# Filter, squared-ReLU layer and slot dispatch on one core: the row path of the dispatch issued later, batch 2 loaded later, probe matmuls left out

## The chip, the cores and the metric

One Trainium2 chip, one of its cores. The metric is the device time of the program in microseconds (us); each run is one execution.

## What is computed

```python
X = np.fft.rfft(x, axis=1); Y = X * F[None]          # x: 8 x 3072 x 256
y = np.fft.irfft(Y, n=3072, axis=1)                  # 24576 tokens x 256
h = np.maximum(y @ w_in, 0.0)                        # 256 -> 2048
z = h * h @ w_out                                    # 2048 -> 256
logits = z @ phi                                     # 24576 x 32 slots
d = softmax of logits over the tokens; slot_input = d.T @ z
slot_out[e] = relu(slot_input[e] @ w1[e]) @ w2[e]    # 8 experts, 4 slots each
c = softmax of logits over the slots
out = c @ slot_out
```

The softmax over all 24576 tokens is kept running: a maximum, a sum and a rescaled accumulator. The softmax over the slots (here the row path) is finished for each token as soon as its logits are there.

## The kernel before

**Filter.** The transform of a batch is split as 128 x 24. The first stage (`mm_a`, `evac_a`, `store_a`) writes its result S to DRAM; the filter stage (`mm_b`, then products on VectorE in `filt` and sums on GpSimd in `join`) and the inverse stage (`mm_g2`, `evac_g2`, `store_g2`) write G to DRAM. `load_g` reads G into `gin`, `mm_ai` transforms and transposes four token columns, and `lead_ai` (ScalarE) and `rest_ai` (VectorE) leave them in `xo` as a leading part and a residual. Batch 0 runs alone at the start; batches 1 to 7 run beside the layer of the batch before.

**Layer.** Work goes in 384 pairs of hidden tiles, eight pairs to a chunk of 512 tokens. A pair has two halves; a half is six matmuls (L460 to L462, three for each of two contraction tiles) into one bank, p0 or p1, which has no second buffer. `square` frees the bank with a relu on ScalarE (L467). The square itself is ScalarE's for the first half (L469) and GpSimd's for the second (L471). `turn_h` transposes both halves into `hT` on VectorE (L478), and `logit` (L487) sums h times a folded weight into bank L every two pairs.

**Dispatch**, once a chunk of tokens (48 times, `dispatch_events`). `evac_l` copies the logits, `gather` sums them into a bank X, `emax` takes the running maximum (VectorE: mn L542, nm L545), `expo` the exponentials (ScalarE: et L551, sc L554), `turn_l` transposes the logits (lt L562) and releases X, `turn_e` transposes the exponentials (eT L568), `slot_in` multiplies them with `hT` into four banks (L589), and `accum` adds these to the accumulator (ac L605, z L612). The row path is `row_max` (rm L574, cl L575), `row_exp` (ScalarE: ce L596), `row_out` (sm, co L623 to L626) and `store_c`.

**What sets the order.** Everything is issued in the order of the Python code. `pair(P)` runs four quarter steps at the times 2P, 2P + 0.5, 2P + 1 and 2P + 1.5, so a time unit is half a pair. Each step first runs events that need no bank, then three matmuls (after two steps the half's `square`), then the other events that are due. Events lie in streams (dsp for the dispatch, late for `out_events`, fft for the filter) with a time each, and leave a stream in that order:

```python
        def put(t, fn, *a):
            streams[nm].append((t + o, fn, a))
...
                if te > t or (n and (early or hold)):
                    break
                if n > len(free):
```

Five side banks are shared by gather, slot_in, the filter's stages and mm_ai; an event that finds too few holds back those behind it. In a dispatch chunk c the times start from `q = 16 * (c + 1) + 2`. An engine's queue runs in the order of issue, and so does SP's, which issues nearly all DMAs. For batch b the times of the filter come from `when`: the first stage's start and spacing, then the starts of the four filter-stage and the four inverse-stage groups, counted from 96 (b - 1).

At the start, beside batch 0, `warm` and `probe` issue matmuls on constants whose results are not read.

Of the kernel before, what the change touches and what calls it, by code (L numbers as in the profile page):

```python
# [6 lines left out]
F32 = mybir.dt.float32  # L7
F32R = mybir.dt.float32r
# [30 lines left out]
def body(tc, x, cA, cAf, fwd, inv, flt, cst, w_in, w_out, phi, w1, w2, out):  # L39
    nc = tc.nc  # L40
    sync = nc.sync
    act, vec, gps, pe = nc.scalar, nc.vector, nc.gpsimd, nc.tensor

    def pool(name, bufs=1, space=None, side=None):
        kw = {} if space is None else {"space": space}
        p = tc.tile_pool(name=name, bufs=bufs, side=side, **kw)
        return p, p.__enter__()
# [7 lines left out]
    cv_c, cv = pool("cv")  # L55
# [43 lines left out]
    def side():  # L99
        if G["nsd"]:  # L100
            return G["ps"].tile([128, 512], F32, tag="sd", name="sd", bufs=G["nsd"])
        k = free.pop(0)
        p = G["ps"].tile([128, 512], F32, tag=f"s{k}", name="sd")
        taken[id(p)] = k, p
        return p
# [7 lines left out]
    def fft_events(b, pl, put, A0, dA, TB, TG, n, st):  # L113
# [190 lines left out]

        def load_ca():
            vec.memset(st["wz"], 0.0)
            gps.memset(st["wy"], 0.0)
            sync.dma_start(out=st["ca"], in_=cAf)

        def warm(a, n):  # L310
# [3 lines left out]
            for _ in range(n):  # L314
                pe.matmul(p[:, 0:w], a[:, 0:128], a, start=True, stop=True)

        def probe():

            m = st["wz"].bitcast(F32R)
            w = st["wy"].bitcast(F32R)  # L320
            p, p2 = side(), side()
            for a, cols, count in ((w, 512, 10), (m, 512, 6), (w, 256, 12), (w, 384, 6), (w, 128, 12)):
                for _ in range(count):
                    pe.matmul(p[:, 0:cols], a[:, 0:128], m[:, 0:cols], start=True, stop=True)
            for _ in range(4):
                for r, q in enumerate((p, p2)):
                    rows = slice(64 * r, 64 * r + 64)
                    pe.matmul(
                        q, w[rows, 0:128], m[rows, :], start=True, stop=True, tile_position=(64 * r, 0)
                    )  # L330

        if b == 0:

            st["wy"] = cv.tile([128, 128], F32, name="wy", bufs=1)
            st["wz"] = cv.tile([128, 512], F32, tag="wx", name="wz", bufs=1)
            st["ca"] = pl().tile([128, 128], F32, name="ca")
            put(0, load_ca)
            put(0.05, warm, st["wz"], 2)
            put(0.05, warm, st["wz"][:, 0:256], 1)
            put(18.2, warm, st["ca"], 16)  # L340
            put(18.25, probe)
            for sl in range(6):
                put(0.1 * sl + 0.2, load_x, sl)
            for u in range(12):
                put(4.6 + 0.9 * u, mm_a, u)
                put(6.7 + 1.0 * u, evac_a, u)
            for i in range(8):
                T = ST["B0"] + ST["dB"] * i
                put((.7, .75, 15)[i] if i < 3 else T - 6.5, load_c, i)
                put((.8, 9, 15.5)[i] if i < 3 else T - 6.4, load_f, i)  # L350
                put(18 + .1 * i if i < 3 else T - 6, load_s, i)
                put(T, mm_b, i)
                for r in range(2):
                    put(T + 1 + .5 * r, filt, i, r)
                    put(T + 1 + .5 * r, join, i, r)
                put(T + 5, mm_g, i)
                for c in range(4):
                    put(T + 6, evac_g, i, c)
                put(T + 7, store_g, i)
            return  # L360
# [157 lines left out]
    def dispatch_events(c, put):  # L518
        q = 16 * (c + 1) + 2
        st = {}  # L520
# [114 lines left out]
            return evac_l, gather, emax, expo, turn_e, turn_l, slot_in, accum, row_max, row_exp, row_out, store_c  # L635
        put(q + .5, evac_l)
        put(q + 1.5, gather)
        put(q + 2, emax)
        put(q + 2.5, expo)
        put(q + 3.5, turn_l)  # L640
        put(q + 4, turn_e)
        put(q + 4.5, row_max)
        put(q + 5.5, row_exp)
        put(q + 7, row_out)
        put(q + 7.5, slot_in)
        for r in range(4):
            put(q + 9 + .5 * r, accum, r)
        put(q + 13, store_c)


    def f64(t, a, e):
# [122 lines left out]
    def stream(nm, o=0):  # L774
        def put(t, fn, *a):
            streams[nm].append((t + o, fn, a))
        return put
# [67 lines left out]
    with tc.manual_schedule():  # L845
        put, late = stream("fft"), stream("late")
        st = {}
        put0(38, load_const)
        fft_events(0, lambda: first, put0, 0, 0, 0, 0, dict(f=17, u=12, c=4), st)
        out_events(0, st, late)  # L850
        def wput(t, *a):
# [22 lines left out]
        for b in range(1, NB):  # L874
            st = {}
            if b == 1:
                when = (24, 1.1, [45.5, 53.5, 65.5, 77.5], [49.5, 61.5, 69.5, 81.5])
            else:
                when = (-25, 1.5, [1.5, 21.5, 37.5, 53.5], [17.5, 33.5, 49.5, 65.5])
            fft_events(b, lambda: G["fft"], stream("fft", 96 * (b - 1)), *when, dict(f=3, u=8, c=2), st)  # L880
            out_events(b, st, late)
        for c in range(NCH - 1):
            dispatch_events(c, stream("dsp"))
# [4 lines left out]
        for P in range(NP + 2):  # L888
            if P == 9:
                open_fft()  # L890
            if P == 48 * (NB - 1):
                G["fft_c"].__exit__(None, None, None)
                G["w1_c"], w1p = pool("w1p")
                for n in range(6):
                    m = 4 if n < 5 else 2
# [25 lines left out]
        def bank(tag):  # L921
            return G["ps"].tile([128, 512], F32, tag=tag, name="pt")
# [28 lines left out]
        def go(*fns):  # L951
            for fn in fns:
# [3 lines left out]
                cnt[fn.__name__] = g + 1  # L956

        evac_l, gather, emax, expo, turn_e, turn_l, slot_in, accum, row_max, row_exp, row_out, store_c = dispatch_events(NCH - 1, None)
        zt = mlp.tile([128, NE, 8, NS], F32, tag="xo", name="zt", bufs=2)
        gps.memset(zt, 0.0)  # L960
# [18 lines left out]
        for n in range(4):  # L979
            w = NB * N2 // 4  # L980
# [14 lines left out]
        p = bank("s0")  # L995
        for j in range(16):
# [3 lines left out]
                start=(j < 4), stop=(j >= 12), tile_position=(0, 32 * c4),  # L1000
# [3 lines left out]
        p = bank("s1")  # L1004
# [61 lines left out]
        p = bank("s4")  # L1066
# [13 lines left out]
        for g in range(NG):  # L1080
            b, o = divmod(g, N2 // 4)
# [3 lines left out]
            for h in range(2):  # L1085
                p = bank(("s0", "s1", "s2", "s3")[ops % 4]).rearrange("p (a d) -> p a d", d=D)
# [156 lines left out]
```

## Time and profile before

| What | before |
|---|---|
| three runs, median (lowest to highest) | 2109.94 us (2109.88 to 2111.64) |
| profiled execution, its own time | 2109.53 us |
| its span, first to last instruction | 2107.3 us |
| busy: PE, DVE, ACT, POOL | 1975.0, 1231.4, 1044.5, 734.2 us |
| mean granted TensorE clock, share of full | 0.970 |
| DMA | 238.30 MB, mean 113 GB/s |

PE is TensorE's matmuls, DVE VectorE, ACT ScalarE, POOL GpSimd, SP the engine that issues the DMAs. Busy time is time in which an engine executes; idle time in front of an instruction is put down to what ended it. The granted clock has two levels, 1.00 (2.4 GHz) and 0.50 (1.2 GHz); a mean between them says how much of a stretch was at either. PE's records overlap, since matmuls are pipelined: a 512-column matmul is recorded with 0.39 us while its successors start 0.23 us apart.

### The profile page before, as it was taken

To read this page: it belongs to the slowest core of one execution; us is meant where nothing else is said; L and a number is where in the kernel's file an instruction comes from. 1 tells how busy PE (TensorE), PEld (TensorE's weight loads), DVE (VectorE), ACT (ScalarE), POOL (GpSimd) and SP (SyncE) were. 2 spreads that over 40 slices of the span, in tenths; PEclk is the share of its full clock that TensorE was granted. 3 is DMA by queue.
4 is the path that set the end of the run, shared out by engine and by line. 5 is a ranking of instruction groups with operands and counts; after the bars stand their busy time and mean duration, and the time that the engine had idled before them with its cause. 6 is when DMAs were issued, how large, how long until landed. Compare 5 with 4: busy or idle time off the path is not lost.

```text
span 2107.3 us, 44638 instructions
## 1 busy us (share of the span) xinstructions
PE 1975.0 (94%) x18364; PEld 1329.6 (63%) x18364; DVE 1231.4 (58%) x2276; ACT 1044.5 (50%) x1956; POOL 734.2 (35%) x787
## 2 busy tenths in 40 slices
PE   7799989999999999999999999999999999999987
PEld 4376656666666667666666667656666666666546
DVE  3674655665565655666466565566466565555548
ACT  2355545544644446445645446444654444444435
POOL 2424444333433334333433343333433332222224
PEclk8699999999999999999999999999999999999999
DMA  9744444241442324232343324223334213000479
GB/s 278 221 135 137 110 146 146 71 108 46 133 110 71 101 77 137 71 87 66 122 112 80 96 82 137 71 75 79 117 100 97 79 51 132 14 22 14 144 268 381
DMA packets 144539, 238.30 MB, mean 113 GB/s; under 512 B 14160, under 2 KB 96592, under 8 KB 144336
## 3 DMA queue, kind: packets, MB, share of 16 engines
q1 hardware_dynamic: 144048, 235.25, 37.5%
q8 instruction: 145, 2.38, 0.5%
q14 instruction: 58, 0.48, 0.1%
q0 software_dynamic: 288, 0.20, 0.0%
HBM read 154.65 MB, written 80.74 MB: 112 GB/s over the span
## 4 chain that ended last, share of the span: by engine, by line
PE 59%; DVE 14%; ACT 10%; issue 2%; POOL 0%; ACTq 0%; POOLq 0%; DVEq 0%
PE p L460 11%; PE p L462 10%; PE p L461 10%; PE sd L589 9%; PE L L487 8%; DVE hT L478 5%; PE sd L406 4%; ACT h L467 3%; ACT f L212 2%; PE sd L202 2%; ACT h L469 2%; DVE u L263 2%; DVE lt L562 2%; ACT et L551 1%; DVE mn L542 1%
## 5 line engine op out<-in xcount | busy, mean ns | idle before, releaser
L478 DVE STREAM_TRANSPOSE hT<-h 128x512 f32<-128x512 f32 x768 | 516.0, 695 | 427.0 <-ACT h L469 425.4
L471 POOL TENSOR_TENSOR h<-h 128x512 f32<-128x512 f32 x383 | 399.1, 1042 | 977.9 <-ACT h L467 872.3
L460 PE MATMUL p<-xo,wiH 128*128 128x512 f32 x1536 | 643.9, 419 | 71.6 <-ACT h L467 70.9
L467 ACT ACTIVATE h<-p 128x512 f32<-128x512 f32 x768 | 453.8, 595 | 514.2 <-PE p L462 492.8
L461 PE MATMUL p<-xo,wiH 128*128 128x512 f32 x1536 | 615.3, 401 | 0.2 <-DVE xo L427 0.2
L462 PE MATMUL p<-xo,wiL 128*128 128x512 f32 x1536 | 614.9, 400 | 0.0
L460 PEld LDWEIGHTS p<-xo,wiH 128*128 128x128 f32 x1536 | 292.8, 191 | 232.7 <-ACT h L467 114.2
L462 PEld LDWEIGHTS p<-xo,wiL 128*128 128x128 f32 x1536 | 293.5, 191 | 71.5
L461 PEld LDWEIGHTS p<-xo,wiH 128*128 128x128 f32 x1536 | 294.2, 192 | 57.2 <-DVE xo L427 0.8
L469 ACT ACTIVATE h<-h 128x512 f32<-128x512 f32 x385 | 243.4, 632 | 12.3
L605 DVE SCALAR_TENSOR_TENSOR ac<-ac,sc,sd 128x512 f32<-128x512 f32 x188 | 132.3, 725 | 180.9 <-PE sd L589 180.9
L272 POOL TENSOR_TENSOR u<-u 128x256 f32<-128x256 f32 x256 | 183.8, 742 | 143.8 <-DVE u L263 135.2
L589 PE MATMUL sd<-hT,eT 32*32 32x512 f32 x6144 | 216.6, 604 | 2.9 <-DVE eT L568 2.9
L487 PE MATMUL L<-h,wf 128*32 128x512 f32 x1536 | 190.9, 609 | 0.4 <-ACT h L469 0.4
L263 DVE TENSOR_TENSOR u<-sd,f 128x512 f32<-128x512 f32 x256 | 161.6, 677 | 29.3 <-PE sd L252 23.0
L589 PEld LDWEIGHTS sd<-hT,eT 32*32 32x32 f32 x6144 | 102.3, 103 | 113.2 <-issue 61.2
L137 POOL TENSOR_TENSOR u<-f,u 128x512 fp32r<-128x512 f32 x84 | 108.3, 1290 | 128.7 <-ACT u L136 119.6
L529 DVE TENSOR_TENSOR lo<-L,lp 128x512 fp32r<-128x512 f32 x48 | 33.1, 690 | 136.4 <-ACT lp L528 136.4
L406 PEld LDWEIGHTS sd<-cst_t,gin 128*128 128x128 f32 x768 | 101.0, 192 | 17.7 <-issue 6.8
L406 PE MATMUL sd<-cst_t,gin 128*128 128x128 f32 x768 | 102.1, 276 | 8.2 <-DMA gin<-G 8.2
L487 PEld LDWEIGHTS L<-h,wf 128*32 128x32 f32 x1536 | 40.8, 112 | 102.8 <-issue 100.9
L212 ACT ACTIVATE f<-sd 128x512 f32<-128x512 f32 x112 | 61.3, 611 | 88.5 <-PE sd L202 88.5
(118 smaller groups left out, 1528.7 us busy)
## 6 DMA issues: line engine op xcount, KB each, us to landing
f<-flt SPq DMA_DIRECT2D x28, 1024.0 KB, 5.7
f<-x SPq DMA_DIRECT2D x48, 512.0 KB, 4.2
S<-u SPq DMA_DIRECT2D x96, 256.0 KB, 2.1
f<-S SPq DMA_DIRECT2D x128, 192.0 KB, 7.3
G<-f SPq DMA_DIRECT2D x128, 192.0 KB, 3.2
gin<-G SPq DMA_DIRECT2D x48, 512.0 KB, 5.2
out<-w1t SPq DMA_DIRECT2D x47, 512.0 KB, 5.1
wx<-w SPq DMA_DIRECT2D x34, 256.0 KB, 5.3
```

The costliest lines, as they stand in the source:

```text
L263: vec.tensor_tensor(out=u, in0=p.rearrange("p (h d) -> p h d", d=D), in1=f[:, 2 * r + k:2 * r + k + 1, :].to_broadcast([128, 2, D]), op=AL ...
L272: gps.tensor_tensor(out=a[:, h, :], in0=a[:, h, :], in1=b[:, 1 - h, :], op=ALU.add if h else ALU.subtract)
L406: pe.matmul(p[:, 128 * a:128 * a + 128], t[:, a, 128 * k:128 * k + 128], cI, start=True, stop=True,)
L460: pe.matmul(p, wh, x[:, 0, kk, :], start=(kk == 0), stop=False)
L461: pe.matmul(p, wh, x[:, 1, kk, :], start=False, stop=False)
L462: pe.matmul(p, wl, x[:, 0, kk, :], start=False, stop=(kk == 1))
L467: act.activation(out=h, in_=p, func=ACTF.Relu, scale=2.0 ** -8)
L469: act.activation(out=h, in_=h, func=ACTF.Square)
L471: gps.tensor_tensor(out=h, in0=h, in1=h, op=ALU.mult)
L478: vec.transpose(hT[c][:, 2 * i + k, :], h2[P, k])
L487: pe.matmul(lg[c][32 * n:32 * n + 32, :], wf[:, f, :], h2.pop((P + n // 2, n % 2)), start=(f < 4), stop=(f >= FT - 4), tile_position=(0, 3 ...
L589: pe.matmul(S[r][32 * t:32 * t + 32, :], e[rows, o:o + 32], h[rows, :, o:o + 32], start=(a == 0), stop=(a == 3), tile_position=(32 * r, 32 ...
```

## The change

Three things are changed.

- In each of the 47 dispatch chunks that run beside the layer, `emax` moves from q+2 to q+2.5, `expo` from q+2.5 to q+3.5, `turn_l` from q+3.5 to q+4, `turn_e` from q+4 to q+5.5; `row_max` from q+4.5 to q+11, `row_exp` from q+5.5 to q+13, `row_out` from q+7 to q+14, `store_c` from q+13 to q+17. `slot_in` and `accum` stay.
- Batch 2 (the third) gets times of its own: its first stage starts at -14 with one step a unit instead of -25 and one in 1.5, and with it its loads of x; its first filter-stage group is at 5.5 instead of 1.5. Of batch 1 the last filter-stage group moves from 77.5 to 76.5 and the third inverse-stage group from 69.5 to 70.5.
- The 54 matmuls of `probe` and the tile they use are left out.

```diff
@@ -304,7 +304,6 @@
 
         def load_ca():
             vec.memset(st["wz"], 0.0)
-            gps.memset(st["wy"], 0.0)
             sync.dma_start(out=st["ca"], in_=cAf)
 
         def warm(a, n):
@@ -314,31 +313,14 @@
             for _ in range(n):
                 pe.matmul(p[:, 0:w], a[:, 0:128], a, start=True, stop=True)
 
-        def probe():
-
-            m = st["wz"].bitcast(F32R)
-            w = st["wy"].bitcast(F32R)
-            p, p2 = side(), side()
-            for a, cols, count in ((w, 512, 10), (m, 512, 6), (w, 256, 12), (w, 384, 6), (w, 128, 12)):
-                for _ in range(count):
-                    pe.matmul(p[:, 0:cols], a[:, 0:128], m[:, 0:cols], start=True, stop=True)
-            for _ in range(4):
-                for r, q in enumerate((p, p2)):
-                    rows = slice(64 * r, 64 * r + 64)
-                    pe.matmul(
-                        q, w[rows, 0:128], m[rows, :], start=True, stop=True, tile_position=(64 * r, 0)
-                    )
-
         if b == 0:
 
-            st["wy"] = cv.tile([128, 128], F32, name="wy", bufs=1)
             st["wz"] = cv.tile([128, 512], F32, tag="wx", name="wz", bufs=1)
             st["ca"] = pl().tile([128, 128], F32, name="ca")
             put(0, load_ca)
             put(0.05, warm, st["wz"], 2)
             put(0.05, warm, st["wz"][:, 0:256], 1)
             put(18.2, warm, st["ca"], 16)
-            put(18.25, probe)
             for sl in range(6):
                 put(0.1 * sl + 0.2, load_x, sl)
             for u in range(12):
@@ -635,17 +617,17 @@
             return evac_l, gather, emax, expo, turn_e, turn_l, slot_in, accum, row_max, row_exp, row_out, store_c
         put(q + .5, evac_l)
         put(q + 1.5, gather)
-        put(q + 2, emax)
-        put(q + 2.5, expo)
-        put(q + 3.5, turn_l)
-        put(q + 4, turn_e)
-        put(q + 4.5, row_max)
-        put(q + 5.5, row_exp)
-        put(q + 7, row_out)
+        put(q + 2.5, emax)
+        put(q + 3.5, expo)
+        put(q + 4, turn_l)
+        put(q + 5.5, turn_e)
         put(q + 7.5, slot_in)
         for r in range(4):
             put(q + 9 + .5 * r, accum, r)
-        put(q + 13, store_c)
+        put(q + 11, row_max)
+        put(q + 13, row_exp)
+        put(q + 14, row_out)
+        put(q + 17, store_c)
 
 
     def f64(t, a, e):
@@ -874,7 +856,9 @@
         for b in range(1, NB):
             st = {}
             if b == 1:
-                when = (24, 1.1, [45.5, 53.5, 65.5, 77.5], [49.5, 61.5, 69.5, 81.5])
+                when = (24, 1.1, [45.5, 53.5, 65.5, 76.5], [49.5, 61.5, 70.5, 81.5])
+            elif b == 2:
+                when = (-14, 1, [5.5, 21.5, 37.5, 53.5], [17.5, 33.5, 49.5, 65.5])
             else:
                 when = (-25, 1.5, [1.5, 21.5, 37.5, 53.5], [17.5, 33.5, 49.5, 65.5])
             fft_events(b, lambda: G["fft"], stream("fft", 96 * (b - 1)), *when, dict(f=3, u=8, c=2), st)
```

Line numbers behind the first hunks are 16 to 18 lower in the changed program: L467 is L449, L551 is L533, L596 is L578, L478 is L460 and L574 is L556 there.

ScalarE around the exponentials, in the chunk that the rows below show at 1932 to 1944 us. h is the layer's hidden tile, p its bank; et and sc are the exponentials, ce the row path's. Before:

```order
L467 ACTIVATE h<-p 128x512
L469 ACTIVATE h<-h 128x512
L467 ACTIVATE h<-p 128x512
L551 ACTIVATE et,zb<-sd,nm 128x512
L554 ACTIVATE sc<-mn,nm 128x1
L467 ACTIVATE h<-p 128x512
L469 ACTIVATE h<-h 128x512
L467 ACTIVATE h<-p 128x512 x2
L469 ACTIVATE h<-h 128x512
L596 ACTIVATE ce<-cl 128x128
L467 ACTIVATE h<-p 128x512 x2
```

and now:

```order
L449 ACTIVATE h<-p 128x512
L451 ACTIVATE h<-h 128x512
L449 ACTIVATE h<-p 128x512 x2
L451 ACTIVATE h<-h 128x512
L533 ACTIVATE et,zb<-sd,nm 128x512
L536 ACTIVATE sc<-mn,nm 128x1
L449 ACTIVATE h<-p 128x512 x2
L451 ACTIVATE h<-h 128x512
L449 ACTIVATE h<-p 128x512 x2
```

The first half's relu and square of the pair now stand ahead of the exponentials, and the row path's exponential is out of this stretch.

VectorE in the same chunk, from the first transposes after the maximum to the start of the accumulation (before), and from the end of the accumulation on (now). lt and eT are transposed logits and exponentials, rm, cl, sm, co the row path, ac and z the accumulation, xo the residual for the next chunk. Before:

```order
L478 STREAM_TRANSPOSE hT<-h 128x512
L562 STREAM_TRANSPOSE lt<-sd 32x128 x4
L478 STREAM_TRANSPOSE hT<-h 128x512
L568 STREAM_TRANSPOSE eT<-et 128x512
L574 TENSOR_REDUCE rm<-lt 128x4
L575 TENSOR_TENSOR cl<-lt,rm 128x128
L478 STREAM_TRANSPOSE hT<-h 128x512 x2
L623 TENSOR_REDUCE sm<-ce 128x4
L624 TENSOR_SCALAR sm<-sm 128x4
L625 RECIPROCAL sm<-sm 128x4
L626 TENSOR_TENSOR co<-ce,sm 128x128
L478 STREAM_TRANSPOSE hT<-h 128x512 x2
```

and now:

```order
L587 SCALAR_TENSOR_TENSOR ac<-ac,sc,sd 128x512 x2
L594 SCALAR_TENSOR_TENSOR z<-z,sc,zb 128x1
L409 TENSOR_TENSOR xo<-sd,xo 128x4x4x32
L556 TENSOR_REDUCE rm<-lt 128x4
L557 TENSOR_TENSOR cl<-lt,rm 128x128
L460 STREAM_TRANSPOSE hT<-h 128x512
L409 TENSOR_TENSOR xo<-sd,xo 128x4x4x32
L460 STREAM_TRANSPOSE hT<-h 128x512 x3
L605 TENSOR_REDUCE sm<-ce 128x4
L606 TENSOR_SCALAR sm<-sm 128x4
L607 RECIPROCAL sm<-sm 128x4
L608 TENSOR_TENSOR co<-ce,sm 128x128
```

The six instructions of the row path stood between the transposes ahead of the accumulation; they now stand behind it, two between the residuals and four behind three more transposes.

SP's queue around the load of `gin` for batch 0's last group (chunk 3), where the f tiles are the filter's large buffers. Before:

```order
L130 DMA f_2762<-x 128x1024 x2
L174 DMA fw<-fwd 48x256 x4
L182 DMA f_2943<-flt 128x2x1024
L130 DMA f_2945<-x 128x1024
L224 DMA G<-f_2893 48x4x256 x4
L190 DMA f_2959<-S 48x4x256 x4
L392 DMA gin<-G 128x1024
```

and now:

```order
L178 DMA iv<-inv 128x256 x2
L174 DMA fw<-fwd 48x256 x4
L182 DMA f_2845<-flt 128x2x1024
L190 DMA f_2856<-S 48x4x256 x4
L374 DMA gin<-G 128x1024
L224 DMA G<-f_2836 48x4x256 x4
L130 DMA f_3063<-x 128x1024
L178 DMA iv<-inv 128x256 x2
```

Three loads of x and the four stores of G stood ahead of that load of gin in these rows; none of them does now.

## Rows read from the trace of the kernel before

**Rows 1.** List of waits, whole span: engine, line, releaser, us in total, times, longest.

```profile
ACT ce L596 <- DVE cl L575: 90.8, 47, 2.9
...
ACT et L551 <- DVE nm L545: 81.5, 48, 2.5
...
PE p L460 <- ACT h L467: 70.9, 57, 2.3
```

**Rows 2.** Busy time by stretch: bounds, length, busy us of PE, PEld, DVE, ACT, POOL (instructions), clock, DMA share, GB/s.

```profile
269.92:328.69 58.77, 49.82 (x498) 32.86 (x490) 30.18 (x53) 26.44 (x50) 30.40 (x33) 0.94 0.46 143
404.76:444.74 39.98, 37.82 (x411) 25.39 (x403) 25.11 (x46) 18.99 (x35) 13.97 (x16) 1.00 0.37 93
444.74:485.81 41.07, 38.92 (x410) 26.06 (x402) 25.09 (x46) 18.98 (x35) 13.95 (x16) 0.96 0.36 91
1680.54:1721.54 41.00, 38.85 (x410) 26.07 (x403) 25.11 (x46) 18.98 (x35) 13.96 (x16) 0.96 0.15 42
765.80:806.97 41.17, 39.59 (x307) 27.28 (x299) 21.26 (x38) 26.72 (x51) 19.40 (x17) 1.00 0.44 143
806.97:844.66 37.69, 37.69 (x352) 26.27 (x350) 20.47 (x40) 21.86 (x40) 12.32 (x12) 1.00 0.46 127
844.66:881.60 36.94, 35.55 (x346) 24.18 (x338) 23.36 (x45) 16.66 (x30) 13.95 (x16) 1.00 0.24 58
```

**Rows 3.** Timeline in chunk 14: start, length, engine, line, operation, idle before and its releaser.

```profile
737.95 0.72 DVE L575 TENSOR_TENSOR cl<-lt,rm 128x128 f32<-128x128 f32 x1
...
738.71 0.31 ACT L596 ACTIVATE ce<-cl 128x128 f32<-128x128 f32 x1 [2.81 <-DVE cl L575]
...
739.55 0.80 PE L460 MATMUL p<-xo,wiH 128*128 128x512 f32 x1 [2.16 <-ACT h L467]
```

**Rows 4.** Timeline in chunk 45, which has no filter work, q+2 to q+7.

```profile
1937.04 0.40 PE L460 MATMUL p<-xo,wiH 128*128 128x512 f32 x1
...
1937.62 0.69 ACT L551 ACTIVATE et<-sd,nm 128x512 f32<-128x512 f32 x1 [1.66 <-DVE nm L545]
1937.74 0.39 PE L460 MATMUL p<-xo,wiH 128*128 128x512 f32 x1
...
1938.49 0.58 ACT L467 ACTIVATE h<-p 128x512 f32<-128x512 f32 x1
...
1939.12 0.50 PE L460 MATMUL p<-xo,wiH 128*128 128x512 f32 x1 [0.53 <-ACT h L467]
...
1944.36 0.50 PE L460 MATMUL p<-xo,wiH 128*128 128x512 f32 x1 [0.77 <-ACT h L467]
```

**Rows 5.** Timeline in chunk 15, around q+4.

```profile
773.55 0.50 PE L460 MATMUL p<-xo,wiH 128*128 128x512 f32 x1 [1.43 <-ACT h L467]
...
774.07 0.61 ACT L136 ACTIVATE u<-f 128x512 fp32r<-128x512 f32 x1
```

**Rows 6.** Timeline, row path in chunk 45, then residual and a square around q+11 to q+13.

```profile
1942.91 0.24 DVE L574 TENSOR_REDUCE rm<-lt 128x4 f32<-128x128 f32 x1
...
1943.18 0.29 DVE L575 TENSOR_TENSOR cl<-lt,rm 128x128 f32<-128x128 f32 x1
...
1958.50 0.68 DVE L427 TENSOR_TENSOR xo<-sd,xo 128x512 fp32r<-128x512 f32 x1
...
1961.92 0.63 ACT L469 ACTIVATE h<-h 128x512 f32<-128x512 f32 x1
```

**Rows 7.** Timeline of SP in chunk 3, then of PE there.

```profile
290.37 0.35 SPq L130 DMA_DIRECT2D f<-x  x1
...
299.89 0.44 SPq L392 DMA_DIRECT2D gin<-G  x1
...
306.28 2.05 PE L406 MATMUL sd<-cst_t,gin 128*128 128x128 f32 x8 [6.38 <-DMA gin<-G]
```

**Rows 8.** Busy time by stretch, from the probes' end to the first transforms' end.

```profile
28.40:34.00 5.60, 0.00 (x0) 0.01 (x1) 0.00 (x0) 0.05 (x1) 1.26 (x1) 0.90 0.51 139
34.00:43.10 9.10, 8.79 (x112) 3.36 (x120) 4.88 (x8) 0.57 (x3) 4.72 (x7) 0.50 1.08 256
```

## The prediction

> **What bounds the kernel now.** I read the list of waits first, then busy time chunk by chunk, and the timeline only where those two pointed. "Chunk n" is the stretch from q of dispatch chunk n to the next q; q+4 is four time units (two pairs) later. TensorE is busy nearly throughout, so only two things can give time: its pauses, and stretches in which it is granted the lower of its two clock levels (1.2 instead of 2.4 GHz). The list of waits names the pauses: 57 times, 70.9 us in all, the first matmul of a layer waits for a relu of ScalarE that frees its bank [rows 1]. The same list says why ScalarE is late: it stands idle for 90.8 us in 47 waits before `row_exp` (for `cl`) and for 81.5 us in 48 before `expo` (for `nm`). ScalarE takes its queue in order, so the relu behind such an instruction waits with it.
>
> Chunk by chunk [rows 2], length less busy time shows that nothing else is missing: chunk 16 (the stretch from 806.97) is busy for all of its 37.69 us; chunk 6 (404.76) lacks 2.16 and chunk 17 (844.66) 1.39. Chunks 7 and 38 (444.74 and 1680.54) lack the same 2.15 and are 1.09 and 1.02 us longer than chunk 6, at a mean clock of 0.96 against 1.00. Rows 3 show such a pause in chunk 14: VectorE starts `cl` only at 737.95, `row_exp` starts at 738.71 after 2.81 us of waiting, the relu follows, and TensorE resumes at 739.55 after 2.16 us.
>
> **The change part by part**, in us of the profiled execution (2109.53, with a span of 2107.3; the median of the runs is 2109.94, 0.4 above it).
>
> *Row path away from q+4.5 to q+7.* `row_max` now stands at q+11 and `row_exp` two units later, so ScalarE has nothing to wait for at q+5.5. The pause of 2.16, which chunks 6 to 8, 12 to 14 and so on to 36 to 38 have, goes 18 times, each with 0.11 for the restart (the first matmul after a pause is recorded with 0.50, others with 0.39 [rows 4]): 18 x 2.27 = **40.9**.
>
> *The lower clock behind those pauses.* 17 of these 18 chunks (all but chunk 6) have about 3.4 us at the lower level, which begin at the end of the pause (in chunk 14 the matmul after it is recorded with 0.80, not 0.50 [rows 3]); chunk 7 is the first, chunk 38 the last [rows 2]. Chunk 6 has the pause without it, so it costs 41.07 - 39.98 = 1.09. Without the pause I expect none of them: chunk 15 (765.80), whose longest pause is 1.43 [rows 5], keeps a clock of 1.00 [rows 2]. 17 x 1.09 = **18.5**.
>
> *Exponential half a pair later.* Before, ScalarE reached `expo` before `nm` was there and waited 1.66 [rows 4]. Now relu and square of the pair's first half go ahead and `nm` is there in time, but the exponentials (1937.62 to 1938.49, 0.87) stand ahead of the relu of the second half. That relu starts 0.58 + 0.63 + 0.87 = 2.1 after the first, while its half is done 1.40 after (three matmuls take 0.70, by the starts at 1937.04 and 1937.74): 0.7 late. A relu must start 0.63 before its bank is wanted again (1938.49 against 1939.12), and by my estimate 0.2 passes from the last matmul to its signal, so 1.40 - 0.63 - 0.2 = 0.55 is to spare, and about 0.2 stays of the pause of 0.53. The bounds are nothing left and all 0.53 left; I take 0.2, from the rows of the same place. Chunks 40 to 46, the kind of rows 4, gain 0.33 here and 0.77 + 0.11 at q+7: 7 x 1.21 = **8.5**. In the six of chunk 17's kind (5, 11 to 35) a filter product now precedes `emax`; I leave 0.25 of 1.39: with the restart 6 x 1.25 = **7.5**. In the five of chunk 15's kind (9 to 33) a split of x (0.61 [rows 5]) also comes ahead of that relu, so 0.8 stays of 1.43: 5 x 0.65; chunk 39 has no split and gains 2.1: together **5.4**. In chunk 16's kind the same instructions precede that relu as before, only without the wait: nothing. In chunk 6's kind the filter stage's first matmuls, issued at q+3.5, give the relu more room: nothing.
>
> *Chunks 0 to 4.* Of the 70.9 some 5 are left for them (less 18 x 2.16, 7 x 1.30, 6 x 1.39 and 9.3 in the others); I take **4.0**.
>
> *Where the row path goes.* On VectorE `row_max` is two instructions, 0.24 + 0.29, and stands behind the first residual of `xo`, which ends at 1959.18 in rows 6, so `cl` is there by about 1959.7. Even if its second instruction takes 0.72 as in rows 3, it is 1960.2. ScalarE reaches `row_exp` after the square that now stands ahead of it, at 1962.55 [rows 6]: 2.3 to spare. `row_exp` delays one relu by about 0.2 of the 0.55 it has: nothing, with 47 x 0.2 = 9 as the far bound. The second residual, behind `row_max`, is due only at q+14; `row_out` at q+14 has its data a unit before. The store of c moves along SP's queue (47 issues, three units behind `row_out`) past loads of the next chunk and finds its data ready: nothing.
>
> That ScalarE and VectorE never reorder their queues stands in the Trainium skill too (TensorE: Matmul & The Clock Gate, "Architectural detail: the array is 16× 32×32, not 1× 128×128"). Taken alone the rule speaks against the change, since it charges both exponentials to a relu in every chunk; the sum would then be the third rival's. Rows 4 agree with the order, and no run here shows the new places yet.
>
> *Third batch's x nearer.* In chunk 3 (269.92) TensorE loses 58.77 - 49.82 = 8.95 [rows 2], 6.38 of it in one wait for `gin`. SP issued that load only at 299.89; the load of x ahead of it, issued at 290.37, had held the queue [rows 7]. In the new order no load of x stands ahead of that `gin`, so 6.4 goes. Of the other 2.6, waits in the same jam, I take 1.4; and the chunk's clock of 0.94, two stretches like those above, gives 2.2. Against it, the twelve first-stage steps of batch 2 now come one a unit from chunk 4 on. A unit there holds 1.40 + 0.70 of TensorE; on ScalarE 0.6 of relu, half a square (0.3), and 0.6 each for split and eviction, 2.1 as well, with one exponential and four evictions of the inverse stage on top: I expect ScalarE to fall behind by 2 to 3.5. VectorE's filter products of chunk 3 meet the row path: about 1. I take 4 lost (bounds 0 and 10): 10.0 - 4.0 = **6.0**.
>
> *Later last filter stage of batch 1 (76.5, 70.5).* It follows from the later `turn_l` and the row path; its cost is in the 1 above.
>
> *Probes.* TensorE does nothing from their end at 28.4 to 34.0, and by the mean of 0.90 the clock is down from about 32.9, then at 0.50 through the first transforms [rows 8]. The probes fill a wait for data and leave no faster clock behind them; without them the idle stretch is longer and ends at the same load. I take 0; if the return to 2.4 GHz came one stretch earlier or later, 1.1 either way.
>
> **Sum:** 40.9 + 18.5 + 8.5 + 7.5 + 5.4 + 4.0 + 6.0 = 90.8, so 2109.5 - 90.8 = 2018.7, rounded to 2019. If every bound falls well (some 7 of small pauses that I leave, 4 in chunk 4, 1 in chunks 0 to 4) it is 2006.
>
> **The rivals.** *The lower clock stays.* The 17 stretches could belong to that place of the program, the filter stage just before, rather than to the pause; chunk 6 has the pause without one. Against: each begins at the end of a pause. 2018.7 + 18.5 = 2037.
>
> *Batch 2 gives its gain back.* ScalarE's backlog in chunk 4, or VectorE's in chunk 3, delays the blocks of S and stalls the filter stage: 10 to 16 more, about 2032.
>
> *ScalarE's order pays in full.* If no relu has slack, 0.87 + 0.2 is paid in all 47 chunks, 50 in place of the 7 counted: 2062. Against: by rows 4 a relu may start late.
>
> *Same wait, new place: slower.* The accumulations on VectorE wait for `slot_in`'s matmuls, and `row_max` now stands behind them in order. If `cl` comes later than ScalarE's arrival at `row_exp` by more than 0.55, TensorE pauses there instead. The gain of 90.8 is 1.9 a chunk, so the change loses from 2.5 late on, 4.8 later than rows 6 let me expect. At 3.0 late, 47 x 2.45 = 115: 2134.
>
> *It does not do what it says.* The order shows the moves, but the pauses may find another releaser, such as POOL's squares that the logits need: 2109.
>
> **How the numbers follow.** The forecast as summed, 2006 to 2026: 0.76. Lower clock stays 0.06, batch 2 gives back 0.08, ScalarE pays in full 0.04, slower 0.03, no change 0.03. The range runs from the best bounds, 2006, to just past the first rival, 2038, and leaves out the last three and edges. A measurement of this kernel tells about 0.2% (4 us) from no change. Faster 0.94, same 0.03, slower 0.03.
>
> **What would show it.** TensorE's waits for the relu fall from 70.9 us to under 12, none above 1; ScalarE's before `row_exp` nearly vanish and those before `expo` fall below 20; chunks of 6's, 7's and 38's kind are all near 37.7 us, the last before the end near 33.8, at clock 1.00; the 6.4 before the transposes of chunk 3 is gone, and chunk 4 shows a few short pauses. The forecast is wrong if chunks 40 to 46 stay above 34.3 us, if a clock of 0.96 persists in chunk 7's kind, or if ScalarE waits for `cl` at q+13.

## The result and the profile after

The changed kernel takes 1992.15 us (median of four runs, 1990.42 to 1992.27) against 2110.38 for the kernel before beside it (four runs, 2109.88 to 2111.64): a ratio of 0.9437, 95% interval 0.9421 to 0.9453. Forecast were 2019.0 and a range of 2006 to 2038: the direction is right, but the gain is 118 us where 91 were summed. The profiled execution has a span of 1988.6 us and a mean granted clock of 0.983 (before 2107.3 and 0.970).

The list of waits of the changed kernel (engine, line, releaser, us, times, longest); besides the lines named above, L442 is L460 of before, L527 is L545 and L557 is L575:

```profile
PEld p L442 <- ACT h L449: 16.2, 43, 0.9
...
PE p L442 <- ACT h L449: 4.0, 11, 0.4
...
ACT et L533 <- DVE nm L527: 4.4, 7, 2.5
...
ACT ce L578 <- DVE cl L557: 2.4, 1, 2.4
```

All three waits of [rows 1] are nearly gone: ScalarE's 90.8 and 81.5 us, and TensorE's 70.9.

Busy time by stretch, same columns as [rows 2]: chunks 3, 4, 5, 6, 7, 15, 16, 17 and 45 of the changed kernel.

```profile
265.47:305.75 40.28, 40.28 (x475) 27.21 (x467) 28.50 (x53) 19.76 (x36) 20.48 (x25) 1.00 0.49 144
305.75:347.79 42.04, 41.73 (x314) 29.63 (x311) 20.15 (x38) 29.89 (x57) 22.70 (x20) 1.00 0.51 168
347.79:384.93 37.14, 37.14 (x406) 25.44 (x403) 23.86 (x46) 17.40 (x31) 13.90 (x16) 1.00 0.41 97
384.93:422.06 37.13, 37.13 (x410) 25.36 (x402) 23.87 (x46) 19.23 (x35) 13.91 (x16) 1.00 0.38 100
422.06:459.21 37.15, 37.15 (x410) 25.36 (x403) 23.86 (x46) 19.21 (x35) 13.91 (x16) 1.00 0.39 101
720.59:760.06 39.47, 39.06 (x306) 27.43 (x299) 20.96 (x38) 27.00 (x51) 19.45 (x17) 1.00 0.44 149
760.06:797.74 37.68, 37.68 (x351) 26.28 (x349) 20.19 (x40) 22.07 (x40) 12.34 (x12) 1.00 0.43 123
797.74:833.36 35.62, 35.29 (x346) 24.26 (x338) 23.23 (x45) 16.81 (x30) 14.01 (x16) 1.00 0.26 65
1817.70:1851.01 33.31, 33.31 (x279) 22.90 (x275) 19.19 (x38) 17.40 (x31) 8.34 (x9) 1.00 0.14 44
```

Length equals busy time in six of the nine, and all stand at full clock. Against [rows 2], chunk 6 went from 39.98 to 37.13 and chunk 7 from 41.07 to 37.15. The odd thing to see: busy time itself fell, from 37.82 to 37.13 in chunk 6, with the same matmuls (402 start in it in both kernels; the counts in the rows take in those that reach over its edges). That is the first part of what the forecast lacked.

Lengths of all chunks, before less after, in the prediction's groups (us, profiled executions):

| Chunks | forecast | measured |
|---|---|---|
| 6 and the 17 of chunk 7's kind (7, 8, 12 to 14, ... 36 to 38) | 59.4 | 68.9 |
| 15's kind (5) and 39 | 5.4 | 11.0 |
| 16's kind (5) | 0 | 0.0 |
| 17's kind (5, without chunk 5) | 6.2 | 6.5 |
| 40 to 46 | 8.5 | 11.7 |
| 0 to 5 (pauses, batch 2, chunk 5) | 11.3 | 19.3 |
| start and end | 0 | 1.4 |
| sum | 90.8 | 118.8 |

Timeline of the changed kernel in chunk 45, the place of [rows 4]:

```profile
1822.82 0.15 DVE L527 TENSOR_SCALAR nm<-mn 128x1 f32<-128x1 f32 x1
...
1823.30 0.63 ACT L451 ACTIVATE h<-h 128x512 f32<-128x512 f32 x1
...
1823.84 0.67 ACT L533 ACTIVATE et<-sd,nm 128x512 f32<-128x512 f32 x1
...
1824.69 0.58 ACT L449 ACTIVATE h<-p 128x512 f32<-128x512 f32 x1
...
1825.04 0.39 PE L444 MATMUL p<-xo,wiL 128*128 128x512 f32 x1
...
1825.33 0.50 PE L442 MATMUL p<-xo,wiH 128*128 128x512 f32 x1
```

`nm` lands at 1822.97, while ScalarE still has the square ahead; the exponential starts with no wait. The relu behind it delays TensorE to 0.29 us between starts instead of 0.23: 0.06 is left of the 0.53 of before, where the prediction left 0.2.

### The profile page after: what moved, and what is told of

It reads as the page before. It is cut to its first block, busy times and chain, and to the rows that moved or that the text cites. A ratio compares the mean times of both kernels' runs of the same rounds, so it can differ in the third digit from the quotient of the medians.

```text
span 1988.6 us, 44516 instructions
## 1 busy us (share of the span) xinstructions
PE 1925.7 (97%) x18310; PEld 1311.7 (66%) x18310; DVE 1202.4 (60%) x2276; ACT 1054.3 (53%) x1956; POOL 734.8 (37%) x786
## 4 chain that ended last, share of the span: by engine, by line
PE 90%; DVE 3%; DMA 2%; ACT 2%; issue 2%; SPq 0%; ACTq 0%
PE p L442 19%; PE p L444 17%; PE p L443 17%; PE sd L571 11%; PE L L469 9%; PE sd L388 4%; PE sd L252 3%; PE sd L202 3%; PE sd L148 1%; PE sd L149 1%; PE sd L150 1%; PE pt L921 1%; DVE ct L932 1%; DMA f<-S 1%; ACT h L449 1%
## 5 line engine op out<-in xcount | busy, mean ns | idle before, releaser
L449 ACT ACTIVATE h<-p 128x512 f32<-128x512 f32 x768 | 459.3, 599 | 563.0 <-PE p L444 548.5
L460 DVE STREAM_TRANSPOSE hT<-h 128x512 f32<-128x512 f32 x768 | 514.1, 693 | 326.7 <-ACT h L451 323.8
L442 PE MATMUL p<-xo,wiH 128*128 128x512 f32 x1536 | 629.7, 410 | 4.0 <-ACT h L449 4.0
L443 PE MATMUL p<-xo,wiH 128*128 128x512 f32 x1536 | 607.2, 395 | 0.2 <-DVE xo L409 0.2
L444 PE MATMUL p<-xo,wiL 128*128 128x512 f32 x1536 | 607.2, 395 | 0.0
L442 PEld LDWEIGHTS p<-xo,wiH 128*128 128x128 f32 x1536 | 288.7, 188 | 144.8 <-issue 69.7
L444 PEld LDWEIGHTS p<-xo,wiL 128*128 128x128 f32 x1536 | 288.6, 188 | 69.8
L443 PEld LDWEIGHTS p<-xo,wiH 128*128 128x128 f32 x1536 | 289.3, 188 | 58.7 <-DVE xo L409 0.8
L469 PE MATMUL L<-h,wf 128*32 128x512 f32 x1536 | 186.0, 598 | 0.4 <-ACT h L451 0.4
```

Of the source, the lines that this page charges most:

```text
L442: pe.matmul(p, wh, x[:, 0, kk, :], start=(kk == 0), stop=False)
L443: pe.matmul(p, wh, x[:, 1, kk, :], start=False, stop=False)
L444: pe.matmul(p, wl, x[:, 0, kk, :], start=False, stop=(kk == 1))
L449: act.activation(out=h, in_=p, func=ACTF.Relu, scale=2.0 ** -8)
L460: vec.transpose(hT[c][:, 2 * i + k, :], h2[P, k])
L469: pe.matmul(lg[c][32 * n:32 * n + 32, :], wf[:, f, :], h2.pop((P + n // 2, n % 2)), start=(f < 4), stop=(f >= FT - 4), tile_position=(0, 3 ...
```

## Experiments

Ratios are to runs of the kernel before on the same chip, whose median lay between 2110.4 and 2111.8 us from one chip to the next; the times themselves compare only within that. "Kind" names are those of the table. Lengths by chunk, us:

| Kernel | time | ratio (95%) | 6 | 7 | 15 | 17 | 44 | 3 |
|---|---|---|---|---|---|---|---|---|
| before | | 1 | 39.97 | 41.08 | 41.16 | 36.95 | 34.97 | 58.77 |
| changed | 1992.15 | 0.9437 (0.9421 to 0.9453) | 37.13 | 37.15 | 39.47 | 35.62 | 33.31 | 40.28 |
| row path alone | 2058.36 | 0.9754 (0.9739 to 0.9768) | 39.20 | 39.20 | 40.76 | 35.85 | 33.93 | 56.81 |
| exponential alone | 2007.73 | 0.9513 (0.9499 to 0.9527) | 37.15 | 37.14 | 39.46 | 36.42 | 33.29 | 55.95 |
| maximum and exponential, no transposes | 2030.52 | 0.9616 (0.96 to 0.9632) | 38.01 | 38.01 | 39.45 | 37.00 | 33.82 | 58.57 |
| transpose of the exponentials alone | 2069.66 | 0.9802 (0.9787 to 0.9816) | 39.36 | 39.36 | 41.16 | 36.36 | 34.39 | 59.40 |
| changed, old batch times | 2004.73 | 0.9492 (0.9476 to 0.9508) | 37.13 | 37.14 | 39.46 | 35.63 | 33.30 | 56.72 |

**1. The row path alone**, on the kernel before:

```diff
-        put(q + 4.5, row_max)
-        put(q + 5.5, row_exp)
-        put(q + 7, row_out)
...
-        put(q + 13, store_c)
+        put(q + 11, row_max)
+        put(q + 13, row_exp)
+        put(q + 14, row_out)
+        put(q + 17, store_c)
```

> Row path late (q+11 to q+17), everything else as before. Two ways to price a pause of TensorE. Starts: a pause costs the gap between the starts of two matmuls less the usual 0.23 us, that is the idle time that the list of waits shows plus 0.16 (a record of 0.39 overlaps its successor's start by that much) plus 0.11 for the restart. Idle: it costs the listed idle time and 0.11, as the prediction had it. At q+7 the trace of before has 59.3 us by starts and 53.6 by idle time in 35 pauses, with 3.9 for restarts and 17 stretches of lower clock at 1.09. Starts: about 2110.4 - 82 = 2028. Idle: about 2034. The clock is 1.00 in chunks 7 to 38 if the pause makes the lower clock, 0.96 in 17 of them if the place in the program does. ScalarE's wait before row_exp falls from 91 us to near nothing, the one before expo stays near 81.

Measured: 2058.36, some 52 us less than before, not 76 to 82. The pause at q+7 and the lower clock are gone, but chunk 7 stops at 39.20 instead of 37.15. TensorE's waits in this kernel, and chunk 7:

```profile
PE L L487 <- POOL h L471: 19.6, 19, 1.0
PE p L460 <- ACT h L467: 17.6, 22, 1.7
```

```profile
439.80:479.00 39.20, 38.16 (x410) 25.46 (x402) 23.99 (x46) 19.10 (x35) 13.83 (x16) 1.00 0.36 95
```

A wait that was covered took the place of the one removed: the logits at q+7 need GpSimd's square of the last half, 1.03 us late in 19 chunks. So something ahead of the row path is late, too.

**2. The exponential alone** (`emax`, `expo`, `turn_l`, `turn_e` at their new places, row path and the rest as before):

```diff
-        put(q + 2, emax)
-        put(q + 2.5, expo)
-        put(q + 3.5, turn_l)
-        put(q + 4, turn_e)
+        put(q + 2.5, emax)
+        put(q + 3.5, expo)
+        put(q + 4, turn_l)
+        put(q + 5.5, turn_e)
```

> Maximum, exponential and transposes later (q+2.5, q+3.5, q+4, q+5.5), everything else as before. By starts the pauses at q+4 are 19.8 us in 21 and 2.3 for restarts, some 6 of which stay in the changed kernel: about 2110.4 - 16 = 2094. By idle time, as predicted, about 10 goes: 2100. The row path stays, so its pauses at q+7 and the 17 stretches of lower clock should stay as they are; if the later transposes of the logits push row_max back, the pauses there grow and the run is slower than 2100.

Measured: 2007.73, some 103 us less, where 10 to 16 were expected. Chunk 7 is at 37.14, as in the whole change, with the row path still at q+4.5 to q+7. The prediction put the 59.4 us of these 18 chunks down to the row path's place and let the later exponential give nothing there; that was wrong. By their lengths these chunks gain 32.2 us from the row path alone, 69.3 from the later exponential alone and 68.9 from the whole change. So the part of the change that the title leaves out, the later maximum and exponential, carries most of it. Either edit alone removes the pause at q+7; their gains (52 and 103, with 11 for the batches) sum to 166, and overlap by 48.

**3 and 4. What in experiment 2 does it.** `nm` in the kernel before, chunk 14, and what follows from it (ScalarE, then VectorE):

```profile
731.04 0.69 ACT L551 ACTIVATE et<-sd,nm 128x512 f32<-128x512 f32 x1 [1.90 <-DVE nm L545]
...
731.91 0.58 ACT L467 ACTIVATE h<-p 128x512 f32<-128x512 f32 x1
732.52 0.63 ACT L469 ACTIVATE h<-h 128x512 f32<-128x512 f32 x1
...
733.18 0.71 DVE L478 STREAM_TRANSPOSE hT<-h 128x512 f32<-128x512 f32 x1 [2.24 <-ACT h L469]
...
735.73 0.67 DVE L568 STREAM_TRANSPOSE eT<-et 128x512 f32<-128x512 f32 x1
...
737.64 0.28 DVE L574 TENSOR_REDUCE rm<-lt 128x4 f32<-128x128 f32 x1
```

ScalarE waits 1.90 for `nm`; relu and square of the pair come late by that, VectorE's transpose waits 2.24 for the square, and `row_max` stands behind it, the transpose of the exponentials and two filter products. Two runs part the wait from that transpose: run 3 moves `emax` and `expo` only,

```diff
-        put(q + 2, emax)
-        put(q + 2.5, expo)
+        put(q + 2.5, emax)
+        put(q + 3.5, expo)
```

> The kernel before with emax at q+2.5 and expo at q+3.5 alone; turn_l, turn_e and the row path stay in their old places, so on VectorE the exponentials are still transposed ahead of row_max. Theory A (ScalarE's wait for nm is the root: it makes the relu and square late, with them VectorE's transposes, with those row_max): ScalarE's wait before the exponential is gone, cl comes about 1.7 us earlier, and nearly all that the later exponential gave with turn_l and turn_e (103 us) is there: 2005 to 2020, chunk 7's kind 37.1 to 37.6, no stretch at the lower clock. Theory B (the transposes that stood ahead of row_max are the root): turn_e now waits on VectorE for an exponential that ends later, row_max stands behind it, and the pause at q+7 stays near 2.2 us: 2080 to 2100, chunk 7's kind above 40.

run 4 `turn_e` only, behind `row_max`:

```diff
-        put(q + 4, turn_e)
         put(q + 4.5, row_max)
+        put(q + 5.5, turn_e)
```

> The kernel before with turn_e alone moved from q+4 to q+5.5, behind row_max. Theory A: cl comes earlier only by the transpose's own 0.67 us, so the pause of 2.16 shrinks to about 1.5 and what follows of the lower clock may go with it (chunk 15 keeps full clock after 1.43): 18 x 0.67 + 18.5 = 31 less, about 2080; with the lower clock staying 2098; ScalarE's wait for nm stays at about 80 us. Theory B: the pause at q+7 goes nearly whole, 2050 or less, chunk 7's kind 39.2 or less as with the row path moved.

Measured: 2030.52 and 2069.66. With the wait gone, chunk 14 (VectorE, ScalarE, TensorE, then its stretch):

```profile
712.47 0.71 DVE L478 STREAM_TRANSPOSE hT<-h 128x512 f32<-128x512 f32 x1
...
717.08 0.28 DVE L574 TENSOR_REDUCE rm<-lt 128x4 f32<-128x128 f32 x1
717.39 0.74 DVE L575 TENSOR_TENSOR cl<-lt,rm 128x128 f32<-128x128 f32 x1
...
718.16 0.31 ACT L596 ACTIVATE ce<-cl 128x128 f32<-128x128 f32 x1 [0.84 <-DVE cl L575]
...
719.01 0.50 PE L460 MATMUL p<-xo,wiH 128*128 128x512 f32 x1 [0.19 <-ACT h L467]
```

```profile
706.21:744.21 38.00, 37.81 (x410) 25.37 (x402) 25.23 (x46) 19.10 (x35) 14.01 (x16) 1.00 0.21 58
```

From the chunk's start, `cl` begins after 11.18 us (717.39 - 706.21) against 13.16 before (737.95 - 724.79): the transpose no longer waits, and the pause falls from 2.16 to 0.19. With only `turn_e` moved, TensorE's pause in chunk 14 and the chunk:

```profile
729.05 0.50 PE L460 MATMUL p<-xo,wiH 128*128 128x512 f32 x1 [1.55 <-ACT h L467]
```

```profile
714.89:754.27 39.38, 37.83 (x411) 25.38 (x403) 25.10 (x46) 18.99 (x35) 14.00 (x16) 1.00 0.19 56
```

The pause is 0.61 shorter, about the transpose's own 0.67, and the clock stays at 1.00. The 0.61 is what chunk 6 gains (39.97 to 39.36); chunk 7 gains 1.72, the rest of it the 1.09 of the lower clock. Theory B fails both times (it had 2080 to 2100 and 2050 or less). Theory A holds for the cause, but its 2005 to 2020 for the first run was 10 too low: without the move of `turn_e`, 0.87 stays in each of the 18 chunks (38.01 against 37.14), of which only 0.19 is listed as idle. Where the rest of it is, the next views show. Run 3 moves the maximum as well; run 10 puts it back beside the late exponential and loses nothing by it, which speaks for the exponential's place, not the maximum's.

**Logits one slot late.** TensorE and GpSimd in chunk 6, kernel before, then changed kernel (second column: time taken):

```profile
421.12 2.34 PE L487 MATMUL L<-h,wf 128*32 128x512 f32 x16
...
421.32 1.04 POOL L471 TENSOR_TENSOR h<-h 128x512 f32<-128x512 f32 x1
```

```profile
397.85 1.05 POOL L453 TENSOR_TENSOR h<-h 128x512 f32<-128x512 f32 x1
...
398.87 1.93 PE L469 MATMUL L<-h,wf 128*32 128x512 f32 x16
```

The 16 logit matmuls run four side by side: in the changed kernel they start in four groups, at 0, 0.45, 0.88 and 1.31 us. Before, the square of the last half ended at 422.36, 1.24 us after they had begun (in the changed kernel 0.03 after). The matmul that needs it started at 1.29 instead of 0.90, the last one moved to a fifth slot at 1.75, and the 16 took 2.34 against 1.93, with no idle time listed for the matmuls. With `emax` and `expo` alone moved, they still take 2.34. The pause itself, in the kernel before, lost more than its 2.16 listed:

```profile
416.97 0.40 PE L462 MATMUL p<-xo,wiL 128*128 128x512 f32 x1
419.53 0.50 PE L460 MATMUL p<-xo,wiH 128*128 128x512 f32 x1 [2.16 <-ACT h L467]
419.87 0.39 PE L461 MATMUL p<-xo,wiH 128*128 128x512 f32 x1
```

The first matmul after it starts 2.56 after its predecessor's start instead of 0.23, and the next one 0.34 after that, 2.33 + 0.11 = 2.44 in all. With the 0.41 of the logits that is 2.85, chunk 6's gain of 2.84; the prediction had 2.27.

**5. The batch times alone**, on the kernel before:

```diff
-                when = (24, 1.1, [45.5, 53.5, 65.5, 77.5], [49.5, 61.5, 69.5, 81.5])
+                when = (24, 1.1, [45.5, 53.5, 65.5, 76.5], [49.5, 61.5, 70.5, 81.5])
+            elif b == 2:
+                when = (-14, 1, [5.5, 21.5, 37.5, 53.5], [17.5, 33.5, 49.5, 65.5])
```

> Only the times of batches 1 and 2 changed. If the jam on SP's queue is all that costs in chunk 3, chunks 3 and 4 together lose about 15.5 us as in the changed kernel: 2095. By the prediction's 6 it is 2104. The wait of 6.4 us before the transposes of chunk 3 is gone either way.

**6. Batch 2's times without those of batch 1** (the last two added lines of that diff):

> Only batch 2 has its new times; batch 1 keeps 77.5 and 69.5. If the loads of x on SP's queue ahead of gin are the cause, nearly all of the gain of chunk 3 is there: 2095 to 2098, and SP issues the gin of chunk 3 in time. If batch 1's times carry a part of it, 2100 or more.

**7. The whole change with the old batch times** (that diff reversed, on the changed kernel):

> The changed kernel with the old times of batches 1 and 2. The wait for gin in chunk 3 is back. If the parts add up, the time is the changed kernel's and what the batch times gave alone: 1992 + 15 = 2007 by the traces of chunks 3 and 4, 1998 by the prediction's 6. With the row path late, VectorE is crowded at q+11 to q+15 of chunk 3, where the old times put four filter products as well: it may cost up to 3 more.

Measured: 2099.49, a ratio of 0.995 (0.9933 to 0.9966); 2102.4, 0.9962 (0.9947 to 0.9977); 2004.73. Alone the times give about 11 us by the ratio, not 15.5: chunks 3 and 4 do lose 14.5 us, but chunk 5, to which a filter group moves, grows by 2.1. Most of the gain is batch 2's. Run 6 misses its 2095 to 2098, which points to a share of batch 1; the two intervals overlap, but the traces show one. Chunk 3 in run 5, then in run 6:

```profile
270.52:311.25 40.73, 40.18 (x474) 26.81 (x466) 27.63 (x53) 19.71 (x36) 20.27 (x25) 1.00 0.48 144
```

```profile
269.36:313.17 43.81, 41.49 (x474) 27.28 (x466) 27.92 (x53) 19.66 (x36) 21.75 (x26) 1.00 0.44 134
```

Without batch 1's new times the load of `gin` goes out 17.1 us into chunk 3 (10.0 with them), and the chunk is 3.1 longer. Beside the other edits the batch times give about 12 us (12.6 by the times, 11.6 by the ratios). Chunks 3, 4 and 5 of run 7, against the first three stretches of the result:

```profile
266.86:323.58 56.72, 49.52 (x498) 33.17 (x490) 28.91 (x53) 26.45 (x50) 30.39 (x33) 0.94 0.49 151
323.58:361.69 38.11, 38.11 (x354) 26.29 (x350) 19.90 (x40) 23.56 (x44) 12.46 (x12) 1.00 0.50 139
```

```profile
361.69:397.32 35.63, 35.30 (x346) 24.31 (x338) 23.23 (x45) 16.76 (x30) 14.00 (x16) 1.00 0.27 67
```

The three sum to 130.46 here and to 119.46 in the changed kernel: 11.0, most of it 7.20 of pauses and the stretches at the lower clock in chunk 3, whose mean clock is 0.94 here and 1.00 there. Chunks 4 and 5 are longer by work that moved there (eight of the first-stage steps, a filter group), not by pauses: chunk 4 has 0.31 idle, chunk 5 none.

SP's queue in the changed kernel, chunk 3:

```profile
275.02 0.44 SPq L374 DMA_DIRECT2D gin<-G  x1
...
283.60 0.35 SPq L130 DMA_DIRECT2D f<-x  x1
```

The load of `gin` goes out 9.5 us into the chunk instead of 30 [rows 7], and x behind it, as forecast.

**8. The probes alone** (the memset, `probe` and its call, as in the change's diff, left out of the kernel before):

> Only the probes left out. Prediction: nothing, 2110.4 within 1.1. If they held something up at the start (the changed kernel reaches its first layer matmul 0.7 us earlier), 2109.5.

Measured: 2111.3, 1.000 (0.9991 to 1.001): the probes are worth nothing. TensorE's first filter matmuls before, then in the changed kernel:

```profile
34.02 5.09 PE L252 MATMUL sd<-f,fw 48*32 48x256 f32 x64 [5.68 <-issue]
```

```profile
33.36 5.14 PE L252 MATMUL sd<-f,fw 48*32 48x256 f32 x64 [13.44 <-issue]
```

The idle stretch grows from 5.68 to 13.44 us and ends no later, and the transforms take the same time. SP issues the first load of S that these matmuls read at 30.95 and 30.14 us, 3.1 and 3.2 us ahead of them, so it is most likely that load that sets the time; the profile itself names no releaser there.

**9. The old row path in chunks 40 to 46 of the changed kernel:**

```diff
+        late_row = (4.5, 5.5, 7, 13) if c >= 40 else (11, 13, 14, 17)
+        for d, fn in zip(late_row, (row_max, row_exp, row_out, store_c)):
+            put(q + d, fn)
```

> The changed kernel with the row path at its old times in chunks 40 to 46 alone, which have no filter work and a clock of 1.00. It measures what a pause costs: chunk 44 is 33.31 us in the changed kernel. Starts: the chunk grows by the listed idle time plus 0.27. Idle: by the listed idle time plus 0.11. With a pause of 0.8 at q+7 that is 34.38 or 34.22. If nothing waits there any more, since maximum and transposes now come in another order, it stays at 33.31.

Measured: 1992.48, 0.9437, with chunk 44 at 33.29: no pause returns. Once the exponential comes later, the row path's place is free there. What the row path (with the probes) still gives beside a later exponential is run 2 against run 7: 3.0 us by the times, 4.4 by the ratios, whose intervals overlap. The chunks tell more: those of 17's kind take 36.42 against 35.63, 0.8 less in each of six with chunk 5.

**10 to 12. What is left.** `emax` back at q+2 with the exponential at its new place; the first stage of batches 3 to 7 at -24 instead of -25; both:

```diff
-        put(q + 2.5, emax)
+        put(q + 2, emax)
...
-                when = (-25, 1.5, [1.5, 21.5, 37.5, 53.5], [17.5, 33.5, 49.5, 65.5])
+                when = (-24, 1.5, [1.5, 21.5, 37.5, 53.5], [17.5, 33.5, 49.5, 65.5])
```

> The changed kernel with the maximum at q+2 again, the exponential still at q+3.5. In chunks 11 to 35 of the kind of chunk 17 a filter product stands ahead of the maximum, and 0.33 us of pause is left: by starts it is worth about 0.6 in five chunks, so 1989. Rival: the pause is the exponential's own length ahead of the relu, and nothing changes: 1992.

> The changed kernel with the first stage of batches 3 to 7 one unit later (-24 instead of -25). In the chunks of 15's kind the first split of x then no longer stands ahead of the relu behind the exponential, and of the 0.41 us of pause left there nothing stays: by starts 0.6 in five chunks, 1989. Rival: ScalarE stays as full and the pause moves: 1992.

> The changed kernel with emax back at q+2 (the exponential stays at q+3.5) and the first stage of batches 3 to 7 starting at -24 in place of -25. Alone they measured 1989.69 and 1990.63 against 1992.15. If the two gains add (2.5 and 1.5): 1988.2. If the filter products behind the moved emax and the moved splits of x meet in the same chunks (11 to 35): 1989.5 or more.

Measured: 1989.69, 0.9424 (0.941 to 0.9438); 1990.63, 0.9432 (0.9416 to 0.9447); both 1987.01 (1986.33 to 1987.76), 0.9411 (0.9397 to 0.9425). Chunks 15 to 17 with both:

```profile
720.72:758.95 38.23, 38.23 (x304) 26.77 (x296) 20.49 (x38) 27.27 (x51) 18.45 (x17) 1.00 0.46 154
758.95:797.45 38.50, 38.50 (x358) 26.87 (x354) 20.20 (x40) 21.74 (x40) 13.36 (x12) 1.00 0.43 120
797.45:832.64 35.19, 35.19 (x347) 24.25 (x339) 23.21 (x45) 16.79 (x30) 13.92 (x16) 1.00 0.27 66
```

The last pauses, 0.41 and 0.33, are gone; chunk 16 takes some of 15's work. By chunk the gains add: run 10 alone has chunk 17 at 35.20, run 11 alone chunks 15 and 16 at 38.23 and 38.51. The runs of both lie wholly below those of the changed kernel, though the intervals of their ratios touch; alone, neither step is told apart from the change by its ratio, only by its chunks.

## Why the prediction was right or wrong

- **Direction and bound: right.** Pauses and the lower clock were what could be had, and nothing became a new bound: TensorE is busy for 1925.7 of 1988.6 us.
- **Row path, 40.9: right for the whole change, wrong in its cause and its size.** "ScalarE has nothing to wait for at q+5.5" is true of the changed kernel, but the row path was late because the exponential waited for `nm` (runs 2 to 4). The step that failed in the cause is "In chunk 6's kind ... nothing" for the later exponential, with 40.9 + 18.5 for the row path in the same chunks: alone the exponential gives 69.3 there and the row path 32.2. It was luck that this did not spoil the sum: alone, the row path's move would have fallen 27 short of the 59.4, since the logits then wait for GpSimd's square (run 1). The step that failed in the number is "each with 0.11 for the restart": beside 2.16 listed, 0.28 was hidden in the restart and 0.41 in the logits, which makes 2.84 instead of 2.27, 18 x 0.57 = 10 us. The same price, listed idle time and 0.11, is too low in the chunks of 15's kind and in 40 to 46.
- **Lower clock, 18.5: right.** No dispatch chunk beside the layer has any left; chunk 7's kind gained 1.09 more than chunk 6. The run with `turn_e` alone shows that it hangs on the pause, not on the place: pauses of 1.53 to 1.70 there leave full clock in all 18 chunks. That refutes the first rival. It does not make the pause the whole cause: chunk 2 of the kernel before had one of 2.21 and kept the full clock.
- **Exponential, 8.5 + 7.5 + 5.4: too small.** Chunks 40 to 46 gained 1.67 each, not 1.21: 0.06 stays at q+4, not 0.2, and the two pauses hid 0.43 beside the 1.30 listed, not 0.11. In 15's kind 1.69 went instead of 0.65: 0.41 of idle time stays where I left 0.8, another 0.15 of it stood elsewhere in the chunk, and some 0.5 was hidden. 17's kind came out right (1.31 for 1.25), in part by luck: 0.33 of idle time stays where I left 0.25, and 0.25 was hidden, not 0.11.
- **Batch 2, 6.0: too small.** Run 7 against the changed kernel is 11.0 in chunks 3 to 5, where 10.0 - 4.0 was summed; the 4 to be lost did not come. I took work that moves to chunk 4 for a jam; ScalarE's backlog, reckoned at "2 to 3.5", cost 0.31 of idle time. The second rival falls with it.
- **Chunks 0 to 4, 4.0: too small.** With the old batch times (run 7) they gained 6.7.
- **Probes, 0: right** (run 8). The 1.4 us at the start and the end are not explained.
- **The other rivals.** ScalarE's order does not pay in full: one exponential ahead of a relu cost 0.06 in chunk 45. The same wait at q+13 does not arise: the one wait for `cl`, of 2.4 us, is in the last chunk, behind the layer. "No change" named the right releaser, GpSimd's squares, but it holds only without the later exponential (run 1).
- **The range.** Its best bound, 2006, was built from listed idle time and was no floor: the weight loads of the same place showed more. In the kernel before:

```profile
PEld p L460 <- ACT h L467: 114.2, 114, 2.7
```

114.2 us and 114 waits there against 70.9 and 57 for the matmuls [rows 1]. Leaving chunks 0 to 5 and the clock aside, the layer's chunks gained 98.1 - 18.5 = 79.6 us, above the whole 70.9 and below 114.2, so neither list gives the price. The Trainium skill (Perfetto Trace Analysis, "Identifying the Most-Contended Engine") says that the busy share of matmuls is no good measure of how close one is to the limit, since they are pipelined, and names the busy share of the weight loads as one of two things to go by instead. This trace agrees on the matmuls: chunk 6's busy time fell by 0.69 with no matmul less.

## What to carry to other kernels

Follow a wait one step further back than the engine that ends it: an instruction that waits in an in-order queue makes everything behind it late, and the late things reach the next engine's queue and return as a second wait further on. Before pricing two edits apart, ask whether either alone would remove the same pause. Price a pause of pipelined matmuls from start to start, with what comes late behind it, not by its listed idle time.

## What the runs showed of the hardware

- One operand that is late for a group of matmuls side by side costs a whole slot, 0.41 us here, and shows as busy time: 16 matmuls in 2.34 instead of 1.93 us.
- At one and the same place, a pause of 2.15 to 2.31 us was followed by 3.41 us at 1.2 GHz in 17 chunks of 18, one of 1.53 to 1.70 us in none (run 4). The pause alone does not decide it: of the four traces with that pause (before and runs 5, 6 and 8; 2.14 to 2.18 us in chunks 6 and 7), chunk 6 kept the full clock in all but run 8, chunk 7 only in runs 5 and 6. Why stays open.
- At the start TensorE could stand idle for 13.44 us instead of 5.68 without any cost that shows (run 8's ratio is 1.000); most likely a load set the time.
